# Threshold attention and a gated two-layer network on one core: statistics and first-product sums in other rounds, the exchange of rounds' work rearranged

## The chip, the cores and the metric

The kernel runs on one core of a Trainium2 chip. The metric is the device time of one execution in microseconds. Three runs of the kernel before took 986.61, 984.64 and 983.08 us, median 984.64.

The engines are named as in the profile: PE is TensorE's matrix product and PEld its loading of weights, DVE is VectorE, ACT is ScalarE, POOL is GpSimd, and SP is the queue that issues most DMAs. Every engine executes its own instructions in program order, and semaphores order them against the other engines.

## The reference

Two blocks follow each other. The first is attention with a threshold, over 8 batches and 8 heads of 576 tokens of width 64; the second takes the 4608 tokens of width 512 through 1024 hidden values and back.

```
scores = scale * np.matmul(q, k.transpose(0, 1, 3, 2))
thresh = np.max(scores, axis=-1, keepdims=True) - tau
scores = np.where(scores >= thresh, scores, -1000000000.0)
attn = softmax(scores)
x = np.matmul(attn, v), heads side by side, as 4608 x 512
h = x @ w_in                                   # 512 -> 1024
solu = h * softmax(h)
ln = (solu - mean) / np.sqrt(var + 1e-06) * g_ln
out = ln @ w_out                               # 1024 -> 512
```

The softmax of the second block runs over the 1024 hidden values of a token, and so do the mean and the variance.

## The kernel before

**Rounds.** The work is written out by hand as a loop over rounds. There are 144 slots of scores, 18 to a batch: four pairs of heads, two kinds of tokens and two halves, and two slots for the last 64 tokens of the batch (kind 2, "end tokens"). Round n computes slot n. Its steps are the scores on PE (`scores`, L466) into one buffer `s_ps`; the row maxima on DVE (`maxes`, L488, two per round); the threshold on ACT (`ramp`, L503) and the exponentials (`exps`, L512). One round later GpSimd divides by the sums (`normalise`, L519, L520, L522) and DVE transposes the weights into T (`blocks`, L534). After the second of two slots SP sends T to wT (L543, L545). Three rounds after that slot, PE forms the product with v (`attend_steps`, L576), always in an even round of the steady part, into one half of each of the two banks "o"; ACT copies the result to `xh`, or to `xe` for end tokens (`attended`, L609), and DVE clears that half of the banks for the next product (`clear`, L615), since the product adds to what is there.

**The steady part.** From round 30 (`START`) the second block runs between the scores. An odd round holds half of the second product of one tile of 128 tokens (`ff_o`, L948) into the other half of the banks "o"; its output is copied out by ACT (`ff_out`, L966) and stored by SP (`ff_store`, L987). An even round holds a phase of a first product, then a product with v, then another phase.

**A pair of tiles.** Tokens of two tiles a and b go through the first product together, with seven phases in place of eight blocks. This needs sums of weights, made once, and sums of tokens on GpSimd (`sums_a`, L655, L656 ahead of the first phase's round; `sums_b`, L661, L662 later). The seven phases (`phase`, L691) lie two to an even round, the seventh alone in the fourth even round, so a pair takes 8 rounds. After every two batches one tile of end tokens follows (`one_h`, L715, in four rounds, with one sum on GpSimd, L667). Pairs begin in rounds 30, 38, 50, 58, 66, 74, 86, 94, 102, 110, 122, 130, 138 and 146, single tiles in 46, 82, 118 and 154; round 144 is the first without scores, and what follows is the tail.

**The fence.** The two phases of an even round write the same banks with different rows of PE. So that they don't meet, GpSimd sets a small tile `mark` after the last products of the first phase (`fence`, L110), and the second phase waits for it. GpSimd takes this instruction in its program order like any other.

**The steps behind a pair**, counted in rounds from its start: the halves of h are taken from the banks by ACT (`keep_half`, L730), completed with the other bank by DVE, which gives the row maximum hm (`add_half`, L737), and combined (L746); ACT takes the exponential with its sum (`pair_exp`, L751); DVE multiplies (`pair_mul`, L757) and GpSimd inverts the sum (`ff_sum`, L875, L876). `ff_stats` has mean and variance on DVE (L885, L886) and then five small operations on GpSimd (L889 to L896, "rs chain") that turn them into scale and offset. Then ACT makes V (`ff_norm`, L906), DVE the same values in u (`ff_norm2`, L911), SP exchanges parts (`ff_swap`, L922), DVE transposes to uT (`ff_turn`, L932), and the second product can begin.

**Order in a round.** Jobs are entered in three lists. The program of an even round is: the list `begin`; scores, maxima, thresholds and exponentials; `normalise` of the slot before; the list `middle`; the phases, the fence and the product with v; `blocks` of the slot before; the list `late`; preparation of later heads (scaling L195, copies L201, transposes L209). Since `middle` comes before the phases, what stands in it on GpSimd is ahead of the fence there. `r + n` below is round n of a pair that began in round r; round 8 of a pair is usually round 0 of the next.

## Time and profile before

| | |
|---|---|
| runs | 986.61, 984.64, 983.08 us |
| profiled execution | 984.76 us, span 983.0 us, 1.8 us around it |
| mean granted TensorE clock | 0.961 |
| busy share | PE 85%, DVE 70%, ACT 61%, POOL 58% |
| first score of round 30 to that of round 38 | 174.02 to 221.13 us |
| last score | 891.4 us; the tail lasts to 983.0 |

In a list of waits a line names the waiting engine, what it was to write and its line in the kernel, what released it, and then the total, the number and the longest of the waits in us. In a timeline a line gives the start and the length in us, engine, line, operation, what it writes and reads, and the size; in brackets stands the idle time ahead of it and what ended it. Where several instructions of a kind are joined, "x16" counts them. A product counts two records per multiplication here. In a table by stretch each line is a stretch of time, its length, the busy time of PE, PEld, DVE, ACT and POOL with the number of instructions, the granted TensorE clock (1.00 is full speed), the busy share of the DMA engines and GB/s.

### The profile page before, as it was taken

To read this page: it belongs to the slowest core of one execution; us is meant where nothing else is said; L and a number is where in the kernel's file an instruction comes from. 1 tells how busy PE (TensorE), PEld (TensorE's weight loads), DVE (VectorE), ACT (ScalarE), POOL (GpSimd) and SP (SyncE) were. 2 spreads that over 40 slices of the span, in tenths; PEclk is the share of its full clock that TensorE was granted. 3 is DMA by queue.
4 is the path that set the end of the run, shared out by engine and by line. 5 is a ranking of instruction groups with operands and counts; after the bars stand their busy time and mean duration, and the time that the engine had idled before them with its cause. 6 is when DMAs were issued, how large, how long until landed. Compare 5 with 4: busy or idle time off the path is not lost.

```text
span 983.0 us, 36466 instructions
## 1 busy us (share of the span) xinstructions
PE 838.3 (85%) x15329; PEld 535.9 (55%) x15329; DVE 691.7 (70%) x1403; ACT 599.2 (61%) x1209; POOL 566.2 (58%) x1022
## 2 busy tenths in 40 slices
PE   5668898887978988888987988988888898988996
PEld 3456566543564555555564554555564465555553
DVE  5968788577685776969687677687778577676251
ACT  5868776566664665757665666566666566664131
POOL 3868578647465465756556456475755557565120
PEclk9879999897999999999999999999999999999998
DMA  9999878776766667675767567766687575545111
GB/s 273 251 244 233 206 180 224 196 169 153 197 169 164 168 166 198 174 205 143 211 175 186 150 168 174 186 172 187 163 233 173 142 172 136 155 102 137 35 45 43
DMA packets 83811, 168.57 MB, mean 171 GB/s; under 512 B 15544, under 2 KB 45248, under 8 KB 83648
## 3 DMA queue, kind: packets, MB, share of 16 engines
q1 hardware_dynamic: 82512, 164.25, 65.5%
q8 instruction: 120, 1.97, 0.9%
q10 hardware_dynamic: 1136, 2.00, 0.6%
q14 instruction: 43, 0.35, 0.1%
HBM read 46.14 MB, written 9.44 MB: 57 GB/s over the span
## 4 chain that ended last, share of the span: by engine, by line
PE 38%; DVE 17%; DMA 14%; ACT 9%; issue 9%; POOL 8%; SPq 5%; DVEq 0%; ACTq 0%; POOLq 0%
PE h L691 12%; DMA wT<-T 10%; PE ov L576 8%; PE s_ps L466 6%; DVE w L488 4%; DVE T L534 4%; PE o_ps L948 3%; ACT w L503 3%; DVE bs L885 3%; PE h_ps L841 2%; ACT w L512 2%; PE ov L948 2%; PE h L715 2%; POOL w L522 2%; DVE u L737 2%
## 5 line engine op out<-in xcount | busy, mean ns | idle before, releaser
L488 DVE CUSTOM_DVE_ANT_0 w<-s_ps,tau_t 128x576 f32<-128x576 f32 x282 | 200.8, 749 | 179.5 <-PE s_ps L466 168.9
L503 ACT ACTIVATE w<-s_ps,nth 128x576 f32<-128x576 f32 x282 | 199.3, 742 | 209.5 <-DVE nth L488 203.0
L522 POOL TENSOR_SCALAR w<-w,sm 128x576 f32<-128x576 f32 x288 | 217.8, 768 | 14.3
L512 ACT ACTIVATE w<-w,ntau 128x576 f32<-128x576 f32 x288 | 219.8, 769 | 0.0
L534 DVE STREAM_TRANSPOSE T<-w 128x576 f32<-128x576 f32 x288 | 207.8, 758 | 12.6 <-POOL w L522 10.6
L948 PE MATMUL ov<-w,uT 64*64 64x256 f32 x3456 | 200.4, 376 | 0.0
L466 PE MATMUL s_ps<-kT,qT 64*64 64x512 f32 (+1 forms) x2048 | 173.0, 427 | 16.7 <-ACT w L503 15.4
L948 PEld LDWEIGHTS ov<-w,uT 64*64 64x64 f32 x3456 | 146.3, 133 | 64.6 <-issue 20.5
L576 PE MATMUL ov<-wT,v 64*64 64x128 f32 (+1 forms) x4752 | 141.5, 266 | 42.7 <-ACT ob L966 26.7
L576 PEld LDWEIGHTS ov<-wT,v 64*64 64x64 f32 x4752 | 130.4, 138 | 87.1 <-ACT ob L966 42.7
L519 POOL TENSOR_SCALAR sm<-sm 128x2 f32<-128x2 f32 x144 | 46.3, 322 | 219.7 <-ACT w L512 214.7
L691 PE MATMUL h<-w,xh 64*64 64x512 f32 x896 | 116.2, 623 | 26.1 <-POOL mark L110 15.0
L520 POOL TENSOR_TENSOR sm<-sm,mone 128x2 f32<-128x2 f32 x144 | 103.3, 717 | 12.0
L466 PEld LDWEIGHTS s_ps<-kT,qT 64*64 64x64 f32 x2048 | 70.5, 141 | 53.7 <-ACT w L503 23.2
L691 PEld LDWEIGHTS h<-w,xh 64*64 64x64 f32 x896 | 36.4, 136 | 80.8 <-issue 27.4
L948 PE MATMUL o_ps<-w,uT 64*64 64x256 f32 x1152 | 70.3, 389 | 8.5 <-DVE uT L932 5.4
L906 ACT ACTIVATE V<-u,nb,rs 128x1024 f32<-128x1024 f32 x36 | 44.5, 1236 | 37.3 <-POOL nb L896 27.9
L948 PEld LDWEIGHTS o_ps<-w,uT 64*64 64x64 f32 x1152 | 48.0, 138 | 33.4 <-issue 12.4
L691 PE MATMUL h<-sums,xh 64*64 64x512 f32 x336 | 60.0, 607 | 0.9 <-DVE hm L737 0.5
L691 PE MATMUL h<-k,sum 64*64 64x512 f32 x224 | 58.1, 638 | 0.0
L932 DVE STREAM_TRANSPOSE uT<-V 128x1024 f32<-128x1024 f32 x36 | 43.6, 1212 | 19.2 <-DMA V<-u 13.4
L512 ACT ACTIVATION_READ_ACCUMULATOR w<-w,ntau 128x1 f32 x288 | 56.0, 194 | 0.0
(122 smaller groups left out, 1009.0 us busy)
## 6 DMA issues: line engine op xcount, KB each, us to landing
wT<-T SPq DMA_DIRECT2D x160, 288.0 KB, 6.1
wT<-T SPq DMA_DIRECT2D x64, 576.0 KB, 5.5
V<-u SPq DMA_DIRECT2D x144, 64.0 KB, 2.3
out_dram<-ob SPq DMA_DIRECT2D x71, 128.0 KB, 4.2
q<-in_q_dram SPq DMA_DIRECT2D x24, 288.0 KB, 4.5
qT<-flip SPq DMA_DIRECT2D x48, 144.0 KB, 3.3
q<-in_k_dram SPq DMA_DIRECT2D x24, 288.0 KB, 4.6
kT<-flip SPq DMA_DIRECT2D x48, 144.0 KB, 2.5
```

The source lines that it names most:

```text
L466: nc.tensor.matmul(out=ps[h][ROWS[y], ks], lhsT=lhsT, rhs=d["kT"][ROWS[h], ks], start=True, stop=True,)
L488: nc.vector.tensor_tensor_reduce(out=w, in0=ps[:, 0:S], in1=(zero if loose else tau_t).to_broadcast([P, S]), scale=1.0, scalar=BIG, op0=AL ...
L503: nc.scalar.activation(out=d["w"][x], in_=d["w"][x] if d["loose"] else d["ps"][x][:, 0:S], func=AF.Prelu, bias=d["nth"][x], scale=-1.0, al ...
L512: nc.scalar.activation(out=w, in_=w, func=AF.Exp, bias=ntau, scale=1.0, accum_out=sm[:, x : x + 1])
L519: nc.gpsimd.tensor_scalar(out=sm, in0=sm, scalar1=1e-9, scalar2=None, op0=ALU.add)
L520: nc.gpsimd.tensor_tensor(out=sm, in0=sm, in1=mone, op=ALU.pow)
L522: nc.gpsimd.tensor_scalar(out=w, in0=w, scalar1=sm[:, x : x + 1], scalar2=1.0, op0=ALU.mult, op1=ALU.mult)
L534: nc.vector.transpose(out=T[:, :, r, h, :], in_=w)
L576: nc.tensor.matmul(out=to, lhsT=d["v"][ROWS[u], (h0 + h - u) % 4 if b > 1 else h0 + h, m ^ 4 * u if m < 8 and b < 2 else m,], rhs=rhs, sta ...
L691: mm = nc.tensor.matmul(out=h[ROWS[y], 512 * bank : 512 * bank + 512], lhsT=x[ROWS[r], ROWS[y]], rhs=w[ROWS[r]], start=c == 0 and (n, r, k ...
L906: nc.scalar.activation(out=V, in_=u, func=AF.Identity, bias=nb, scale=rs)
L948: nc.tensor.matmul(out=d["o"][ROWS[z], of : of + 256], lhsT=d["uT"][ROWS[r], m].rearrange("p y x -> p (y x)"), rhs=w2[ROWS[r], m ^ r, 256 ...
```

## The change

- The product with v is drawn from a list of its own (`pv`), of which an even round takes 36 multiplications (72 for end tokens) and the odd round after it the rest. The copy to xh or xe moves to the head of the `begin` list of a later round. `ready`, which lets a pair start, is set so that pairs start in the same rounds.
- The banks are no longer cleared. The first product with v after a new second product has begun in the banks adds to them without a start flag (`both["open"]`), and other products with v begin with one.
- A single phase in an even round (round 6 of a pair, and the second part of a single tile) comes ahead of the product with v.
- `blocks` comes directly behind `normalise`, ahead of `middle`.
- `sums_a` has three operations and moves to `late` of round 0, behind the fence; `sums_b` has one. The third sum, `s2`, shares a buffer with `ident` and `swapped`.
- Copies from the banks and exponentials move to `begin` lists, additions and `pair_mul` to `middle`.
- `ff_stats(a)` moves from `middle` of round 7 to `middle` of round 8, `ff_stats(b)` from round 9 to round 10; norms are in rounds 9 and 12, turns in late 10 and 14. In a single tile the exponential moves to `begin` of round 3.
- `hm` of the halves has two buffers instead of three.

```diff
@@ attend_steps
+        unit["within"] = "open" in both
+        if unit["within"]:
+            assert both["open"] == "fresh"
+            both["open"] = "used"
...
-                            start=m == 0 and "o" not in both, stop=m == NK - 1,
-                            skip_group_check="o" in both,
+                            start=m == 0 and not unit["within"], stop=m == NK - 1,
+                            skip_group_check=unit["within"],
@@ sums
+        both["s2"] = work.tile([P, 2, P], F32, tag="ident", bufs=1, name="sum")
         nc.gpsimd.tensor_tensor(out=both["s"], in0=x2[:, 0:2], in1=x2[:, 2:4], op=ALU.add)
+        nc.gpsimd.tensor_tensor(out=both["s2"], in0=both["s"], in1=x1[:, 0:2], op=ALU.subtract)
         nc.gpsimd.tensor_tensor(out=x2[:, 0:2], in0=x2[:, 0:2], in1=x1[:, 0:2], op=ALU.subtract)
     def sums_b(ts):
-        x1 = tokens(ts[0])
-        nc.gpsimd.tensor_tensor(out=x1[:, 0:2], in0=both["s"], in1=x1[:, 0:2], op=ALU.subtract)
-        nc.gpsimd.tensor_tensor(out=x1[:, 2:4], in0=x1[:, 2:4], in1=x1[:, 0:2], op=ALU.subtract)
+        x = tokens(ts[0])[:, 2:4]
+        nc.gpsimd.tensor_tensor(out=x, in0=x, in1=both["s2"], op=ALU.subtract)
@@ new_pair
-        at(late, 1, first)
-        at(late, 3, second)
-        at(late, 5, lambda: (add_half(a, 1, 1), add_half(b, 1, 0), pair_exp(a)))
-        at(late, 6, lambda: (pair_mul(a), ff_sum(a)))
-        at(middle, 7, lambda: ff_stats(a))
-        at(late, 7, lambda: (keep_half(b, 0, 1), add_half(b, 0, 0), pair_exp(b)))
-        at(begin, 8, lambda: ff_norm(a))
-        at(middle, 8, lambda: (ff_norm2(a), ff_swap(a)))
-        at(late, 8, lambda: (pair_mul(b), ff_sum(b)))
-        at(middle, 9, lambda: ff_stats(b))
-        at(late, 9, lambda: ff_turn(a, r + 9))
-        at(begin, 10, lambda: ff_norm(b))
-        at(middle, 10, lambda: (ff_norm2(b), ff_swap(b)))
-        at(late, 14 if r + 14 <= NS else 11, lambda: ff_turn(b, rnd))
+        at(late, 0, lambda: sums_a(ts))
+        at(begin, 1, first)
+        at(middle, 1, lambda: add_half(a, 0, 1))
+        at(late, 1, lambda: sums_b(ts))
+        at(begin, 3, second)
+        at(middle, 5, lambda: (add_half(a, 1, 1), add_half(b, 1, 0), pair_max(a)))
+        at(begin, 6, lambda: pair_exp(a))
+        at(begin, 7, lambda: keep_half(b, 0, 1))
+        at(middle, 7, lambda: (add_half(b, 0, 0), pair_max(b), pair_mul(a), ff_sum(a)))
+        at(begin, 8, lambda: pair_exp(b))
+        at(middle, 8, lambda: (ff_stats(a), pair_mul(b), ff_sum(b)))
+        at(begin, 9, lambda: ff_norm(a))
+        at(middle, 9, lambda: (ff_norm2(a), ff_swap(a)))
+        at(middle, 10, lambda: ff_stats(b))
+        at(late, 10, lambda: ff_turn(a, rnd))
+        at(begin, 12, lambda: ff_norm(b))
+        at(middle, 12, lambda: (ff_norm2(b), ff_swap(b)))
+        at(late, 14, lambda: ff_turn(b, rnd))
@@ new_one
-        at(late, 2, lambda: (ff_max(t), ff_exp(t)))
-        at(late, 3, lambda: (ff_mul(t), ff_sum(t)))
+        at(late, 2, lambda: ff_max(t))
+        at(begin, 3, lambda: ff_exp(t))
+        at(middle, 3, lambda: (ff_mul(t), ff_sum(t)))
         at(middle, 4, lambda: ff_stats(t))
...
+        at(late, 10 if r < NS else 8, lambda: ff_turn(t, rnd))
@@ o_steps, steady_round
+            if m == 0 and ffn[t]["otag"] is None:
+                both["open"] = "fresh"
             if m + n == 2 * NC:
+                both.pop("open", None)
...
+        pv = []
+        def attend_some(n):
+            key, steps = pv[0]
+            if sum(1 for _ in zip(range(n), steps)) < n or n > 144:
+                pv.clear()
+                begin.setdefault(rnd + 1, []).insert(0, lambda: done_with(key))
         def steady_round(due):
             if (rnd - START) % 2:
+                if pv:
+                    attend_some(145)
                 o_steps(NC)
                 return
...
                     new_pair(ts, rnd)
-                    sums_a(ts)
...
                     new_one(ts[0], rnd)
                     sum_one(ts[0])
...
-            if steps[1:] or steps and rnd >= NS:
+            if steps:
                 steps[0]()
             if due:
                 key = pv_due.pop(0)[1]
-                for _ in attend_steps(key):
-                    pass
-                done_with(key)
-                late.setdefault(rnd + 1, []).append(clear)
+                pv.append((key, attend_steps(key)))
+                attend_some(72 if key[1] == 2 else 36)
             elif rnd >= NS:
                 o_steps(NC // 2 if steps else NC)
-            if steps and rnd < NS or steps[1:]:
-                steps[-1]()
+            if steps[1:]:
+                steps[1]()
@@ the loop over rounds
             if rnd - 1 in live:
                 normalise(rnd - 1)
+                if rnd >= START:
+                    blocks(rnd - 1)
```

More of the change, by code (lines that the diff above doesn't have):

```diff
@@ L66 @@
     small = ctx.enter_context(tc.tile_pool(name="small", bufs=3))
+    signs = work.tile([P, 2 * P], F32, tag="ident", bufs=1, name="ident")
+    ident, swapped = signs[:, 0:P], signs[:, P : P + 64]
     ps_mm = ctx.enter_context(tc.tile_pool(name="ps_mm", bufs=1, space=PSUM))
-    ident = const.tile([P, P], F32, name="ident")
-    swapped = const.tile([P, 64], F32, name="swapped")
     w1 = const.tile([P, NP, DFF], F32, name="w1")
@@ L611, in attended @@
             pairs_free.append(tag)
-    def clear():
-        nc.vector.memset(both["o"].rearrange("p (u n) -> p u n", u=2)[:, :, 0:P], 0.0)
     both = {}
@@ L678, in product @@
             5: lambda: (both["s"][:, c], seven[0, c]),
-            6: lambda: (x1[:, c], seven[1, c]),
+            6: lambda: (both["s2"][:, c], seven[1, c]),
             7: lambda: (x2[:, c], block(0, 1, c)),
@@ L733, in add_half @@
         d = ffn[t]
-        m = small.tile([P, 1], F32, tag=f"hm{g}", name="hm")
+        m = small.tile([P, 1], F32, tag=f"hm{g}", bufs=2, name="hm")
         d["m"].append(m)
@@ L740, in add_half, with pair_max @@
         )
-    def pair_exp(t):
+    def pair_max(t):
         d = ffn[t]
         m, n = d["m"]
-        nm = small.tile([P, 1], F32, tag="hm", name="hm")
+        d["nm"] = nm = small.tile([P, 1], F32, tag="hm", name="hm")
         nc.vector.tensor_scalar(
@@ L748, in pair_exp @@
         )
+    def pair_exp(t):
+        d = ffn[t]
         d["u"] = new_u()
@@ L751, in pair_exp @@
         nc.scalar.activation(
-            out=d["u"], in_=d["x"], func=AF.Exp, bias=nm, scale=1.0, accum_out=d["se"]
+            out=d["u"], in_=d["x"], func=AF.Exp, bias=d["nm"], scale=1.0, accum_out=d["se"]
         )
@@ L770, in first @@
             keep_half(a, 0, 0)
-            add_half(a, 0, 1)
-            sums_b(ts)
         def second():
@@ L797, in at @@
             when.setdefault(r + n, []).append(job)
-        at(late, 2, lambda: (ff_max(t), ff_exp(t)))
-        at(late, 3, lambda: (ff_mul(t), ff_sum(t)))
+        at(late, 2, lambda: ff_max(t))
+        at(begin, 3, lambda: ff_exp(t))
+        at(middle, 3, lambda: (ff_mul(t), ff_sum(t)))
         at(middle, 4, lambda: ff_stats(t))
-        if r < NS:
-            at(begin, 7, lambda: ff_norm(t))
-            at(middle, 7, lambda: (ff_norm2(t), ff_swap(t)))
-            at(late, 10, lambda: ff_turn(t, rnd))
-        else:
-            at(begin, 5, lambda: ff_norm(t))
-            at(middle, 5, lambda: (ff_norm2(t), ff_swap(t)))
-            at(late, 6, lambda: ff_turn(t, rnd))
+        n = 7
+        at(begin, n, lambda: ff_norm(t))
+        at(middle, n, lambda: (ff_norm2(t), ff_swap(t)))
+        at(late, 10 if r < NS else 8, lambda: ff_turn(t, rnd))
         oq.append(t)
@@ L1106, in done_with @@
             if kind == 2 and b % 2:
-                ready.append((rnd + 1, [(b // 2,)]))
+                ready.append((rnd + (rnd < START), [(b // 2,)]))
             elif kind < 2 and hp == NP - 1:
-                ready.append((rnd + 1, [(b, kind, 0), (b, kind, 1)]))
+                ready.append((rnd + (rnd < START), [(b, kind, 0), (b, kind, 1)]))
         def o_steps(n):
@@ L1144, in steady_round @@
                     sum_one(ts[0])
-                    hsteps.append([lambda t=ts[0]: None, lambda t=ts[0]: one_h(t, 0)])
+                    hsteps.append([lambda: None, lambda t=ts[0]: one_h(t, 0)])
                     hsteps.append([lambda t=ts[0]: one_h(t, 1)])
             steps = hsteps.pop(0) if hsteps else []
-            if steps[1:] or steps and rnd >= NS:
+            if steps:
                 steps[0]()
@@ L1162 @@
             if not more and not (
-                ready or cur or prev or between or pv_due or live or oq or hsteps or ojob
+                ready or cur or prev or between or pv_due or live or oq or hsteps or ojob or pv
                 or max([rnd - 1, *begin, *middle, *late]) >= rnd
@@ L1172 @@
                 both["h"], both["o"] = take("h2")[1], take("ov")[1]
-                clear()
                 oq.append(prev)
```

## The prediction

> **What bounds the kernel now.** I read the page's busy shares first, then TensorE's waits, then the timeline around two beginnings of a pair, and last a table by stretch. The steady part (rounds 30 to 143) decides.

> The page's first part, and then TensorE's waits (us in total, times, longest):

> ```profile
> PE 838.3 (85%) x15329; PEld 535.9 (55%) x15329; DVE 691.7 (70%) x1403; ACT 599.2 (61%) x1209; POOL 566.2 (58%) x1022
> ```

> ```profile
> PE h L691 <- DVE hm L737: 29.2, 24, 2.0
> PE ov L576 <- ACT ob L966: 26.7, 15, 2.9
> PE s_ps L466 <- ACT w L503: 16.3, 18, 2.4
> PE h L691 <- POOL mark L110: 15.0, 11, 3.4
> ...
> PE ov L576 <- DMA wT<-T: 9.6, 14, 2.0
> ...
> PE o_ps L948 <- DVE uT L932: 5.4, 2, 5.0
> PE h L691 <- ACT u L730: 4.7, 13, 0.4
> PE ov L576 <- DVE ov L615: 3.5, 3, 1.4
> ```

> TensorE is busy 85% and is the only engine without slack; what it waits for is short and many-sided. The change aims at hm, ob, wT and ov. The line to watch is the fourth: the fence on GpSimd, only 15.0 us now.

> An ordinary beginning of a pair (round 74, from 454.46), from the timeline:

> ```profile
> 454.46 1.16 PE L466 MATMUL s_ps<-kT,qT 64*64 64x64 f32 x16
> 456.10 0.24 POOL L201 COPY qe<-qT 128x64 f32<-128x64 f32 x1
> 457.37 0.72 DVE L488 CUSTOM_DVE_ANT_0 w<-s_ps,tau_t 128x576 f32<-128x576 f32 x1
> 460.82 0.09 POOL L110 MEMSET mark<- 128x1 f32 x1
> 460.96 1.95 PE L691 MATMUL h<-w,xh 64*64 64x512 f32 x16 [0.65 <-POOL mark L110]
> 461.56 1.18 DVE L757 TENSOR_TENSOR u<-u 128x1024 f32<-128x1024 f32 x1
> 461.84 1.00 POOL L201 COPY qe<-qT 128x64 f32<-128x64 f32 x1
> ```

> The one beginning in which the statistics of an earlier tile stand ahead of the fence (round 86, from 531.18):

> ```profile
> 534.43 1.28 DVE L885 BATCH_NORM_STATS2 bs<-u 128x6 f32<-128x512 f32 x2
> 536.07 0.34 POOL L889 TENSOR_SCALAR rs<-mv,se 128x1 f32<-128x1 f32 x1 [0.96 <-DVE mv L886]
> 537.75 0.26 POOL L896 TENSOR_SCALAR nb<-mv,rs 128x1 f32<-128x1 f32 x1
> 539.44 0.10 POOL L110 MEMSET mark<- 128x1 f32 x1
> 539.59 3.25 PE L691 MATMUL h<-w,xh 64*64 64x512 f32 x16 [3.38 <-POOL mark L110]
> 542.59 1.60 PE L466 MATMUL s_ps<-kT,qT 64*64 64x64 f32 x16
> ```

> Here GpSimd waits for DVE's mv, does five small operations and two sums, and only then sets the mark. TensorE stands 3.38 us, and the next phase takes 3.25 us where 1.95 is usual. The table by stretch says why (time; PE, PEld, DVE, ACT, POOL busy; granted clock; DMA):

> ```profile
> 536.20:539.50 3.30, 0.01 (x2) 0.00 (x0) 1.06 (x2) 0.94 (x3) 2.87 (x8) 1.00 0.34 69
> 540.10:543.50 3.40, 3.40 (x28) 1.22 (x24) 0.00 (x0) 0.00 (x0) 3.13 (x6) 0.50 0.94 252
> ```

> After the standstill the granted clock is 0.50 for one stretch of about 3.4 us: from this phase (539.59) to the second product (which starts at 544.02) it takes 4.43 us instead of 1.77+0.97 = 2.74, so a long wait costs another 1.7 us.

> **The change, part by part.** The unit is a pair of token tiles: 8 rounds. From starts of undisturbed instructions in the timeline: scores 0.97, phase 1.77, product with v 1.96, half a second product 3.45. So 8×0.97 + 7×1.77 + 4×1.96 + 4×3.45 = 41.8 us without waits. Measured from score start to score start: seven ordinary periods 49.48, 49.29, 50.54, 52.8, 48.54, 49.52, 48.15, mean 49.8; the first after a single tile 53.0, 51.3, 51.1, mean 51.8; single tiles (21.6 without waits) 29.0, 26.2, 26.2, mean 27.1; rounds 30 to 38 47.1, rounds 38 to 46 52.6.

> *The split.* An even round asks for 36 multiplications of a unit that has 9×2×2 = 36 (72 of 72 for the end tokens; the profile counts two records each): the whole product stays in the even round and the odd one only finds the end. What really moves is the copy to xh or xe: to the head of ScalarE's next even round, where it waits for the half second product before it. The pairs begin at the same rounds. I price it between −1 and +1 us a pair and take 0: 0.37 us of copy beside 0.97 of scores and 1.77 of a phase, which cover it.

> *No clearing.* 60 memsets of 0.272 = 16.3 us of DVE go; only the 3.5 us wait on L615 was on the path.

> *Order in a round.* The phase of round 6 and the single tile's product now come ahead of the product with v and cover its wait for ob (26.7 us in 15). T directly behind the normalising sends wT's DMAs ahead of the middle list (1.4 us by stats and T), past nothing but itself on SP; the 12 us on wT goes. Copies and exponentials at a round's begin and the additions in the middle list end most of hm: 0.6 a pair is left (1.94 in the rows of round 2). All this is the gain: 49.8 − 41.8 = 8.0 a pair now, of which 0.7 stays (0.6 hm, 0.1 in round 6).

> *Sums.* One operation (0.73) more ahead, one less behind, and all three behind the fence: 0.7 to 1.4 us off GpSimd ahead of the mark. This is inside the next step.

> *Statistics in even rounds: the cost.* stats(a) moves from round 7 to round 0 of the next pair, stats(b) from round 1 to round 2. There GpSimd does normalise, the rs chain, the reciprocal of the sums, and then the fence that the second phase waits for. Round 0, from its score start E: DVE begins its maxes at E+2.7 (457.37−454.46 = 2.91 now; the list it carries from round 7 is alike), maxes 1.36, T 1.42, stats 1.49: mv at E+7.0. pair_mul (1.18) follows on DVE at once. While it runs GpSimd stands: L201 took 1.00 beside it and 0.24 without it. So the chain (0.34+0.23+0.58+0.19+0.26 with gaps, 536.07 to 538.01 = 1.94) begins about 0.8 late or at its end, 8.15; it ends at 10.1, the two operations on se 0.8, mark 0.1: E+10.9. Naturally TensorE is there at 0.97+1.77+1.96 = E+4.7. Wait 6.2; bounds 3.6 (the row of round 86 with its 0.18 of pipelined end) and 7. Round 2 has a lighter list and no pair_mul: maxes from E+2.2, then 1.36+1.42+1.49+0.11+1.94+0.1 = E+8.6 against 4.7 and 0.6 of hm: 3.3; bounds 0 and 3.6. The slow stretch behind: 1.7 in round 0, and 1.3 in round 2, a wait nearer to one stretch, where not every alignment is punished (3.10 at 310.95 was: 3.31 us for the phase; 2.87 and 2.68 elsewhere were not).

> [...]

> *Ordinary period after:* 41.8 + 0.7 + 6.2 + 1.7 + 3.3 + 1.3 = 55.0, against 49.8: +5.2, eight times (58, 66, 74, 94, 102, 110, 130, 138) = +41.6. Rounds 38 to 46: 55.0 − 52.6 = +2.4. First after a single tile: its statistics stand in round 0, without pair_mul, and nothing in round 2: 41.8 + 4.3 + 1.7 + 1.0 = 48.8, −3.0, three times = −9.0. Single tile: its sum comes behind the same chain (10.8 + 0.73 = E+11.5), and its product needs it at 0.97+1.96+1.1 = E+4.0: wait 7.5, 21.6+7.5+1.7 = 30.8 against 27.1, three times = +11.1. Rounds 30 to 38 have no statistics ahead: −3 (0 to −5.3). Tail: −5 (0 to −10): the last tile's 5.02 us wait for uT and its slow product shrink.

> Later turns (10, 14), norms (9, 12), two hm buffers and the shared buffer of ident cost 0: the tiles' second products begin in the same rounds, covered by 8 rounds of lag; without that cover an uT wait of 1.2 a tile.

> Sum: 41.6+2.4−9.0+11.1−3−5 = +38.1. Against the profiled execution's 984.76 us (span 983.0, 1.8 around it, 0.1 above the median of the runs): 1022.9, taken as 1023.

> **The rivals.**
> *R1, faster: the fence waits only as the row of round 86 does (3.6 + 1.7) and not at all in round 2*, because DVE, 16 us lighter and with lists spread, gets to its maxes early. Period 41.8+0.7+5.3 = 47.8 (−2.0×8), rounds 38 to 46 −4.8, first after single −3.7×3, single 26.8 (−0.3×3), −3, −5: −41, 944. For it: that row is the only direct one. Against it: there GpSimd waited for one tile's statistics with DVE early (533.10, E+1.9), without pair_mul or se. It decides where fence waits and slow stretches of an ordinary pair come to less than 8.3 us instead of my 12.5 (9 periods of 42.5+X against 451.0, others +5.9 lower).
> *R2, a trade:* X near 8.3: 976 to 1002, about 985.
> *R3, worse:* both waits at their upper bounds and both punished in full, X = 7+3.6+1.7+1.7 = 14, the single tiles +1 each: 1039 and more, up to 1060 if the copy at the head of the even round holds the maxes' ramps too.
> *The split is real* (half of a product lands in the odd round): then even rounds are 1 us shorter ahead of the fence and the wait is 1 longer: the same time.

> **How the numbers follow.** My forecast 0.68, its own range 1003 to 1036; R1 0.17 (932 to 975); R2 0.07; R3 0.08. The range of 8 in 10 takes my case, R2 and the nearer part of R1: 968 to 1037. About 0.3% (3 us) is what a measurement can tell from no change. Slower: 0.68+0.08+0.01 = 0.77; same 0.04 (the middle of R2); faster 0.17+0.02 = 0.19.

> **What would show it.** TensorE's waits: fence about 95 us (15.0 now), the single tile's product on its sum about 20, hm about 6, ob and wT next to none, no L615 memset; granted clock 0.5 behind the fence in most even rounds 0. Wrong if the fence stays under 50 us, if DVE's maxes in round 0 begin before E+1.5, or if hm stays where it is.

## The result, and the profile after

The changed kernel takes 1025.43 us (median; 1021.05 to 1030.83) beside 983.86 us (979.69 to 986.61) for the kernel before: 1.0429 times as long, 95% interval 1.0354 to 1.0504. The profiled execution took 1021.31 us with a span of 1019.5, that is 36.5 us more span than before; the sum on record said 38.1. Two kernels below, the one with statistics in odd rounds and the one with T early in odd rounds as well, were profiled in a slower execution than most of theirs (932.67 us beside a median of 919.88, and 995.30 beside 985.88), so I use waits and lengths of rounds of these two profiles, and no total time.

TensorE's longest waits in the changed kernel, from the list of waits:

```profile
PE h L694 <- POOL mark L110: 80.9, 22, 5.7
PE s_ps L466 <- ACT w L503: 18.3, 19, 3.1
PE h L718 <- POOL sum L670: 12.0, 4, 4.7
PE ov L582 <- ACT ob L971: 10.8, 9, 1.6
PE ov L582 <- DMA wT<-T: 6.2, 9, 2.1
...
PE h L694 <- DVE hm L740: 2.5, 3, 1.1
```

The many short waits of before are mostly gone (hm 29.2 to 2.5, ob 26.7 to 10.8), and one wait has grown past all of them: the fence, 15.0 to 80.9 us.

The beginning of the pair of round 66 (408.42), from the timeline:

```profile
410.77 0.72 DVE L488 CUSTOM_DVE_ANT_0 w<-s_ps,tau_t 128x576 f32<-128x576 f32 x1
...
412.10 1.43 DVE L534 STREAM_TRANSPOSE T<-w 128x576 f32<-128x576 f32 x2
...
413.46 1.24 DVE L890 BATCH_NORM_STATS2 bs<-u 128x6 f32<-128x512 f32 x2
...
414.86 1.17 DVE L763 TENSOR_TENSOR u<-u 128x1024 f32<-128x1024 f32 x1
415.05 1.20 POOL L894 TENSOR_SCALAR rs<-mv,se 128x1 f32<-128x1 f32 x1 [2.42 <-DVE mv L891]
...
418.78 0.10 POOL L110 MEMSET mark<- 128x1 f32 x1
...
418.93 3.69 PE L694 MATMUL h<-w,xh 64*64 64x512 f32 x16 [5.21 <-POOL mark L110]
```

Maxes, T and statistics stand one behind the other on DVE; GpSimd waits 2.42 us for mv, then needs 3.7 us to the mark, and TensorE waits 5.21 us in all. The table by stretch (columns as before) gives the clock after it:

```profile
418.05:424.88 6.83, 5.95 (x40) 2.13 (x44) 0.30 (x1) 1.67 (x2) 6.40 (x13) 0.50 0.22 60
```

From the spans and records I worked out, for the rounds with scores from 30 on (174.6 to 933.4 us in the profile after), how long TensorE was idle and how much of its busy time lay in stretches at 0.50, half of which counts as lost: idle 93.7 to 122.3 us, lost to the clock 17.1 to 37.4 us, the rest 606.5 to 599.1. So 41.4 us more there: 28.6 of waiting, 20.3 of clock, 7.4 given back. A phase takes 1.95 us by its records and 1.77 from start to start, so 0.18 us of its end is covered where no gap follows; 33 fewer gaps (89 to 56) would by this be 6 of the 7.4, an estimate.

### The profile page after: what moved, and what is told of

Read it like the earlier page. It is cut to its first block, busy times and chain, and to the rows that moved or that the text cites. A ratio compares the mean times of both kernels' runs of the same rounds, so it can differ in the third digit from the quotient of the medians.

```text
span 1019.5 us, 36371 instructions
## 1 busy us (share of the span) xinstructions
PE 846.6 (83%) x15329; PEld 523.6 (51%) x15329; DVE 670.9 (66%) x1343; ACT 600.8 (59%) x1209; POOL 560.6 (55%) x1022
## 4 chain that ended last, share of the span: by engine, by line
PE 39%; DVE 22%; POOL 10%; DMA 10%; ACT 9%; issue 7%; SPq 2%; DVEq 0%; ACTq 0%; POOLq 0%
PE h L694 12%; PE s_ps L466 8%; DVE T L534 7%; PE ov L953 7%; DMA wT<-T 6%; DVE w L488 5%; ACT w L503 3%; ACT w L512 3%; PE o_ps L953 3%; PE ov L582 3%; DVE bs L890 3%; PE h_ps L846 2%; POOL rs L894 2%; DMA v<-in_v_dram 2%; POOL rs L898 2%
## 5 line engine op out<-in xcount | busy, mean ns | idle before, releaser
L488 DVE CUSTOM_DVE_ANT_0 w<-s_ps,tau_t 128x576 f32<-128x576 f32 x282 | 201.6, 751 | 267.1 <-PE s_ps L466 218.1
L503 ACT ACTIVATE w<-s_ps,nth 128x576 f32<-128x576 f32 x282 | 199.8, 743 | 148.2 <-DVE nth L488 144.4
L522 POOL TENSOR_SCALAR w<-w,sm 128x576 f32<-128x576 f32 x288 | 213.7, 754 | 14.3
L466 PE MATMUL s_ps<-kT,qT 64*64 64x512 f32 (+1 forms) x2048 | 178.3, 435 | 20.0 <-ACT w L503 17.5
L953 PEld LDWEIGHTS ov<-w,uT 64*64 64x64 f32 x3456 | 141.6, 134 | 72.9 <-issue 29.8
L694 PE MATMUL h<-w,xh 64*64 64x512 f32 x896 | 129.4, 694 | 59.4 <-POOL mark L110 57.6
L582 PEld LDWEIGHTS ov<-wT,v 64*64 64x64 f32 x4752 | 126.1, 134 | 62.5 <-issue 26.3
L582 PE MATMUL ov<-wT,v 64*64 64x128 f32 (+1 forms) x4752 | 135.0, 260 | 22.5 <-ACT ob L971 10.8
L466 PEld LDWEIGHTS s_ps<-kT,qT 64*64 64x64 f32 x2048 | 68.1, 146 | 62.7 <-issue 29.5
L694 PEld LDWEIGHTS h<-w,xh 64*64 64x64 f32 x896 | 38.5, 151 | 115.2 <-POOL mark L110 60.1
L733 ACT COPY u<-h 128x512 f32<-128x512 f32 x56 | 31.4, 587 | 111.0 <-PE h L694 111.0
L911 ACT ACTIVATE V<-u,nb,rs 128x1024 f32<-128x1024 f32 x36 | 44.6, 1240 | 53.2 <-POOL nb L901 50.1
L894 POOL TENSOR_SCALAR rs<-mv,se 128x1 f32<-128x1 f32 x36 | 24.8, 689 | 84.3 <-DVE mv L891 84.2
```

Source lines behind the costliest of these rows:

```text
L466: nc.tensor.matmul(out=ps[h][ROWS[y], ks], lhsT=lhsT, rhs=d["kT"][ROWS[h], ks], start=True, stop=True,)
L488: nc.vector.tensor_tensor_reduce(out=w, in0=ps[:, 0:S], in1=(zero if loose else tau_t).to_broadcast([P, S]), scale=1.0, scalar=BIG, op0=AL ...
L503: nc.scalar.activation(out=d["w"][x], in_=d["w"][x] if d["loose"] else d["ps"][x][:, 0:S], func=AF.Prelu, bias=d["nth"][x], scale=-1.0, al ...
L522: nc.gpsimd.tensor_scalar(out=w, in0=w, scalar1=sm[:, x : x + 1], scalar2=1.0, op0=ALU.mult, op1=ALU.mult)
L582: nc.tensor.matmul(out=to, lhsT=d["v"][ROWS[u], (h0 + h - u) % 4 if b > 1 else h0 + h, m ^ 4 * u if m < 8 and b < 2 else m,], rhs=rhs, sta ...
L694: mm = nc.tensor.matmul(out=h[ROWS[y], 512 * bank : 512 * bank + 512], lhsT=x[ROWS[r], ROWS[y]], rhs=w[ROWS[r]], start=c == 0 and (n, r, k ...
```

## The experiments

All ratios are to the kernel before, run beside it on the same chip, with the 95% interval. The medians of the kernel before lie between 980.3 and 984.9 us from one set of runs to the next, so a difference in us between two changed kernels of different sets can be off by some us; the ratios are the better measure there. E is the start of a round's first score, "the mark" the start of the memset that is the fence.

### Statistics alone, in the kernel before

```diff
-        at(middle, 7, lambda: ff_stats(a))
...
-        at(begin, 8, lambda: ff_norm(a))
-        at(middle, 8, lambda: (ff_norm2(a), ff_swap(a)))
+        at(middle, 8, lambda: ff_stats(a))
...
-        at(middle, 9, lambda: ff_stats(b))
...
+        at(begin, 9, lambda: ff_norm(a))
+        at(middle, 9, lambda: (ff_norm2(a), ff_swap(a)))
+        at(middle, 10, lambda: ff_stats(b))
+        at(late, 10, lambda: ff_turn(a, rnd))
...
```

> The kernel before, with only the statistics moved as in the change (statistics of a in round 8, of b in round 10, norms in 9 and 12, turns late in 10 and 14; in the tail the single tile's norm and turn in 7 and 8). My theory (this move alone is enough for the loss): the mark of round 0 comes at about E+9.4 instead of E+6.4, a wait of 4.8 instead of 0.65 and a slow stretch of 1.7 to 2.6, round 2 0.8 more: 5 to 8 us a period, 1025 to 1065 us, fence wait 60 to 100 us. Rival (the loss needs the other parts, above all pair_mul beside the chain or the lists at begin): 975 to 1000.

Measured: 1025.99 us, 1.0454 (1.0399 to 1.0508). The fence leads TensorE's waits:

```profile
PE h L691 <- POOL mark L110: 60.1, 21, 4.5
```

The mark of round 0 comes at E+9.7 (mean of eight pairs; E+6.35 before). The move alone is enough for a loss of the observed size. But the changed kernel has parts that win, as the runs below show, so it needn't be all of the loss there.

### The chain behind the fence

```diff
-        at(middle, 8, lambda: (ff_stats(a), pair_mul(b), ff_sum(b)))
+        at(middle, 8, lambda: (ff_stats(a), pair_mul(b)))
+        at(late, 8, lambda: (ff_chain(a), ff_sum(b)))
...
         at(middle, 10, lambda: ff_stats(b))
+        at(late, 10, lambda: ff_chain(b))
...
         at(middle, 4, lambda: ff_stats(t))
+        at(late, 4, lambda: ff_chain(t))
...
```

`ff_stats` keeps DVE's three operations here, and `ff_chain` has GpSimd's five.

> The changed kernel, with one thing moved: the five small GpSimd operations of the statistics (rs chain) and the reciprocal of the sums stand behind the round's phases and fence (late list) in rounds 8 and 10 of a pair, 4 of a single tile; DVE's part stays. My theory (the fence queued behind the rs chain is the whole loss): TensorE's wait for the fence falls from 80.9 us to under 15, the wait of the single tile's product from 12.0 to under 3, the stretches at granted clock 0.50 behind the fence go, and the time falls to 920 to 955 us, under both kernels. Rival (DVE is the late one and the chain only shows it): fence wait goes, but waits on hm, ob or wT come in its place, 970 to 1000. Rival (the copies and exponentials at a round's begin are the loss): 1000 to 1030.

Measured: 990.4 us, 1.0104 (1.0064 to 1.0144): 35 us less than the change, not 70 to 105. The fence wait is 0.2 us, but this stands at the head of the list:

```profile
PE h L694 <- DVE hm L740: 50.4, 14, 4.8
```

The first rival is what happened, with a chain of its own. From the timeline of this kernel (rounds 58 to 60):

```profile
363.17 1.24 ACT L918 ACTIVATE V<-u,nb,rs 128x1024 f32<-128x1024 f32 x1 [3.60 <-POOL nb L908]
...
369.04 1.50 DVE L534 STREAM_TRANSPOSE T<-w 128x576 f32<-128x576 f32 x2 [6.39 <-POOL w L522]
...
371.16 0.68 DVE L740 CUSTOM_DVE_ANT_0 u<-h,u 128x512 f32<-128x512 f32 x1
...
372.00 1.99 PE L694 MATMUL h<-k,sum 64*64 64x512 f32 x8 [4.59 <-DVE hm L740]
```

Behind the fence GpSimd now does the chain, se and three sums before it normalises slot 58. DVE's T of that slot is the next in its queue and stands 6.39 us; the addition that TensorE needs is queued behind T, although its own input is long there. This made T's early place a suspect.

### pair_mul beside the chain

```diff
-        at(middle, 8, lambda: (ff_stats(a), pair_mul(b), ff_sum(b)))
+        at(middle, 8, lambda: (pair_mul(b), ff_stats(a), ff_sum(b)))
```

> The changed kernel with pair_mul of b ahead of the statistics of a in round 8, no longer beside the rs chain. If DVE's two-input product holds GpSimd's operations (in the changed kernel the first of the chain took 1.20 us beside it), the chain only starts as late as it could go on before: the first operation takes 0.35 again, the mark comes within 0.3 us of where it was, 1018 to 1030 us. If it doesn't hold them: the mark comes 1.2 us later in each of 10 rounds, 1033 to 1040.

Measured: 1026.68 us, 1.0471 (1.039 to 1.0552). The first operation of the chain, in the list of groups, in the change and then in this kernel:

```profile
L894 POOL TENSOR_SCALAR rs<-mv,se 128x1 f32<-128x1 f32 x36 | 24.8, 689 | 84.3 <-DVE mv L891 84.2
```

```profile
L894 POOL TENSOR_SCALAR rs<-mv,se 128x1 f32<-128x1 f32 x36 | 12.6, 350 | 103.3 <-DVE mv L891 103.2
```

It takes 350 ns when pair_mul is out of the way, and the mark comes at E+10.63 instead of E+10.38. Delaying the chain by pair_mul's whole length costs 0.25 us: beside it GpSimd had been held for nearly as long. So the 0.8 us of hold in the prediction's working stands.

### A real split

```diff
-                attend_some(72 if key[1] == 2 else 36)
+                attend_some(36 if key[1] == 2 else 18)
```

> The changed kernel, with 18 (36 for end tokens) multiplications of a product with v in the even round, so that half of it really lands in the odd round. My theory (the even round's fence comes at a time that GpSimd sets; TensorE only waits 1 us longer for it, and the odd round is 1 us longer): fence wait 80.9 + 17 to 25 us, the time the same or up to 12 us more, 1020 to 1037. Rival (a product with v in two parts fills a wait elsewhere): 1005 to 1017.

Measured: 1053.14 us, 1.0728 (1.0668 to 1.0788), 28 us above the change: the direction of the theory, and more than twice its upper bound of 12. The fence wait is 98.6 (+17.7, as expected), the single tile's product waits 17.0 for its sum (+5.0), and the loss to the clock goes from 37.4 to 46.9, which I had left out. The odd rounds of ordinary pairs take 0.9 to 1.3 us more, while rounds 0 and 2, whose ends the fence sets, change by −0.5 and +0.1 only.

### Statistics of b in an odd round

```diff
-        at(middle, 10, lambda: ff_stats(b))
+        at(middle, 11, lambda: ff_stats(b))
```

> The changed kernel with only the statistics of b one round later, in round 11, an odd one without fence. Theory (each statistics ahead of a fence costs what I priced it at): the fence wait in round 2, 2.65 to 2.87 us a pair, and its slow stretch go, 9 to 10 pairs: 25 to 35 us less, 990 to 1002. Rival (the wait moves on to hm, ob or uT, or to the fence of round 4): over 1010.

Measured: 1034.4 us, 1.0537 (1.047 to 1.0605): no gain, and about 9 us more than the change. The wait and slow stretch of round 2 are gone as expected (seven ordinary pairs: idle 2.76 to 0.00 us in rounds 2 and 3), but most of it comes back in the same pairs: 0.98 in rounds 4 and 5, 2.52 instead of 1.22 in rounds 6 and 7, so that an ordinary pair takes 53.9 us instead of 54.4. The rest of the time is lost elsewhere: first pairs after single tiles take 53.2 instead of 50.2, single tiles 30.4 instead of 29.2, the tail 90.1 instead of 86.1; the clock loss is 46.2 instead of 37.4. The rival holds. Part of the way shows in the groups of ScalarE: V of b is at the head of round 12's list and, with its values only made in round 11, all V wait 77.7 us for nb (50.1 in the change); exponentials wait 21.4 us for the DMA of the exchange (10.4). What makes the first pairs and the tail longer stays open.

### The order of the phases, and then T with it, in the kernel before

```diff
-            if steps[1:] or steps and rnd >= NS:
+            if steps:
                 steps[0]()
...
-            if steps and rnd < NS or steps[1:]:
-                steps[-1]()
+            if steps[1:]:
+                steps[1]()
```

> The kernel before, with only the order of the phases taken from the change: the single phase of round 6 and the single tile's second part ahead of the product with v. Theory (the wait for ob, 26.7 us in 15, stands mostly there and is covered by 1.77 us of phase): ob wait under 12 us, time 962 to 976. Rival (the next wait, hm in round 0 or wT, takes the place): 979 to 987.

Measured: 959.42 us, 0.9758 (0.9685 to 0.9831): below the theory's range. ob has gone from TensorE's longer waits; the wait for wT has grown from 9.6 to 21.1. The next kernel has this and, in addition,

```diff
                 normalise(rnd - 1)
+                if rnd >= START:
+                    blocks(rnd - 1)
```

> The kernel before with two parts of the change: the order of the phases (which alone gave 959.4 us and left a wait of 21.1 us for wT and 31.3 for hm) and the transposes T ahead of the middle list. Theory: T and so wT's DMAs go out 1 to 1.5 us earlier, the wait for wT falls under 10 us, hm stays or grows by up to 10 since the middle list comes later on DVE; 945 to 957 us. Rival (T, queued on DVE before the middle list, waits for GpSimd's normalising and holds the statistics, so that fence or hm take all of it): 958 to 970.

Measured: 1000.14 us, 1.019 (1.0125 to 1.0256). The wait for wT is 10.3 us, as hoped, but the time is 41 us more than without T's early place, worse than either theory. The way is the rival's: T stands for GpSimd's normalising 37.6 us in all instead of 10.2, here with T early and then without:

```profile
L534 DVE STREAM_TRANSPOSE T<-w 128x576 f32<-128x576 f32 x288 | 210.4, 765 | 37.6 <-POOL w L522 37.6
```

```profile
L534 DVE STREAM_TRANSPOSE T<-w 128x576 f32<-128x576 f32 x288 | 207.8, 758 | 12.0 <-POOL w L522 10.2 <-DMA V<-u 0.8 <-DMA wT<-T 0.5
```

The statistics stand behind T, the rs chain behind the statistics. The marks of rounds 0 and 2 come at E+7.83 and E+8.00 instead of 6.36 and 6.32, and the fence wait is 25.6 us instead of 4.1.

### T's place in the changed kernel

Taken back in all rounds:

```diff
                 normalise(rnd - 1)
-                if rnd >= START:
-                    blocks(rnd - 1)
```

> The changed kernel with only the transposes T back at their old place, behind the phases and ahead of the late list. Theory (T's 1.42 us of DVE stand ahead of the statistics, which hold the fence): the mark of rounds 0 and 2 comes 1.4 us earlier, fence wait 80.9 to 50 to 62 us, less at granted clock 0.50, against 6 to 15 us more of waits for wT; 990 to 1012 us. Rival (the gain on wT is as large as what T costs the fence, as I priced it): 1018 to 1030.

Measured: 966.3 us, 0.9842 (0.9784 to 0.99): without this one line the change is faster than the kernel before. Its TensorE waits:

```profile
PE h L694 <- POOL mark L110: 49.4, 22, 3.9
PE ov L582 <- DMA wT<-T: 17.1, 28, 2.1
```

The fence waits 31.5 us less, wT 10.9 us more. The marks come at E+8.59 and 6.19 (change: 10.38 and 7.49), and the loss to the clock is 28.3 us (37.4). ob, 10.8 us in the change, is gone from the waits: those of ScalarE's 28 exponentials, of which one of a pair stands ahead of a copy to ob, fall from 34.0 to 10.9 us.

Early in even rounds alone:

```diff
-                if rnd >= START:
+                if rnd >= START and rnd % 2 == 0:
                     blocks(rnd - 1)
```

> The changed kernel with T ahead of the middle list in even rounds only. This tells in which rounds T's early place costs the 59 us that taking it back in all rounds won. Theory (in even rounds T stands directly ahead of the statistics, and the mark comes 1.0 to 1.5 us later in rounds 0 and 2; in odd rounds it only holds the additions, the exponential of round 6 and by it ob): most stays, 1000 to 1018 us, fence wait 65 to 80, ob wait under 4. Rival (odd rounds alone, as in the kernel with statistics in odd rounds, where T there cost 66): 962 to 975.

Measured: 1012.92 us, 1.0336 (1.0277 to 1.0395), fence wait 77.5 us. The marks of rounds 0 and 2 come at E+9.96 and 7.51, 1.4 and 1.3 us later than with T late, as expected. By the ratios, of the 5.9% that T's place costs in the change, 4.9% come from the even rounds, where T stands directly ahead of the statistics; the remaining 1% is no larger than the intervals. The expected end of ob did not come (10.2 us).

### Statistics in odd rounds

```diff
+        at(late, 5, lambda: pair_exp(a))
+        at(late, 6, lambda: (pair_mul(a), ff_sum(a)))
+        at(middle, 7, lambda: (ff_stats(a), add_half(b, 0, 0), pair_max(b)))
+        at(late, 7, lambda: pair_exp(b))
+        at(late, 8, lambda: (pair_mul(b), ff_sum(b)))
+        at(middle, 9, lambda: (ff_norm2(a), ff_swap(a), ff_stats(b)))
...
-                if rnd >= START:
+                if rnd >= START and rnd % 2 == 0:
                     blocks(rnd - 1)
```

(The first addition of a pair stands first in its list, and the single tile's statistics are in round 5; all else is as in the change.)

> The changed kernel with both statistics in odd rounds (a in 7, b in 9, single tile in 5), exponentials and products as early as in the kernel before, the first addition at the head of its list, and T ahead of the middle list in even rounds only; phase order, no clearing, sums behind the fence, norms and turns as in the change. Theory (the rest of the change is sound, and only the statistics ahead of the fence made it slow): fence wait under 15 us, hm under 15, period of a pair 44 to 47 us, 915 to 945 us. Rival (DVE or GpSimd, with 40 us and more of work in a period, set the pace in odd rounds): 950 to 980.

Measured: 919.88 us, 0.9358 (0.9282 to 0.9434): 6.4% less than the kernel before, the fastest here. The fence wait is a little over the expected 15 us:

```profile
PE h L694 <- POOL mark L110: 17.3, 13, 2.0
```

In rounds 0 and 1 of ordinary pairs TensorE is idle 0.08 us and loses nothing to the clock (change: 5.51 and 2.09). With T early in odd rounds as well:

> The kernel with statistics in odd rounds, with T ahead of the middle list in every round as in the change, no longer in even rounds alone. Theory (in odd rounds T sends no DMA and only holds the additions and the statistics, and by them GpSimd and the next fence): fence wait in round 2 from 0.7 to 2.0 us to 2 to 3.5, time 930 to 950 us. Rival (T's place is indifferent where the statistics aren't ahead of a fence): 915 to 925.

Measured: 985.88 us, 1.0059 (1.0019 to 1.0099), 66 us more and 36 above the theory's range. Here the odd rounds hold the statistics, and here T's place costs in the odd rounds: the mark of round 2 comes at E+9.73 instead of 6.51. The fence wait is 42.1 us, and hm, absent before, 14.5: the additions stand behind T as well. With the run before this shows what matters: not even or odd, but T ahead of what a fence, or a phase, waits for in the end.

### A dose on the fence

Six idle operations on GpSimd are put ahead of the fence of round 0, in the kernel with statistics in odd rounds:

```diff
+    def slow_pool():
+        for _ in range(6):
+            nc.gpsimd.tensor_tensor(out=mark, in0=mone[:, 0:1], in1=mone[:, 0:1], op=ALU.pow)
...
+        at(middle, 8, slow_pool)
```

> The kernel with statistics in odd rounds, with six idle operations of 0.57 us on GpSimd (about 3.9 us start to start) in the middle list of round 8 of each pair, that is ahead of the fence of a next pair's round 0 (twelve times in the rounds with scores): a dose of the delay alone, on a kernel in which DVE and ScalarE are as early as can be. Theory (late fence and slow stretch behind it are the cost, 3.4 to 3.9 us of wait and 1.3 to 2.6 of clock each): 45 to 80 us more, 965 to 1000. Rival (other engines catch up in the wait, and the rest of the period gives it back): under 955.

Measured: 986.66 us, 1.0034 (0.9992 to 1.0077), 67 us more. One of the places, from the timeline:

```profile
348.42 4.26 POOL L767 TENSOR_TENSOR mark<-mone 128x1 f32<-128x1 f32 x6
352.75 0.10 POOL L110 MEMSET mark<- 128x1 f32 x1
...
352.90 2.95 PE L694 MATMUL h<-w,xh 64*64 64x512 f32 x16 [3.89 <-POOL mark L110]
```

In ordinary pairs rounds 0 and 1 have 3.84 us of idle time (0.08 without the dose) and lose 1.82 us to the clock (0): 5.6 us each, and twelve of them would be 67. Rounds 2 to 7 of these pairs are idle as long as without the dose (3.75 and 3.76 us), so nothing is given back there. That the product meets the difference so exactly is partly luck: three of the doses fall on single tiles, which take 27.7 us instead of 23.1, and the pairs behind those take 44.8 instead of 46.9. For a wait of 3.8 us, the price that the prediction used, the wait plus one slow stretch, is right.

## Why the prediction was right, and where it was not

**Right by its main mechanism.** The fence is queued behind the statistics' chain on GpSimd, TensorE waits for it in rounds 0 and 2 of each pair, and behind the longer wait the granted clock is 0.50 (at 418.05 to 424.88, behind 5.21 us). The dose measures the price alone; the chain behind the fence ends the fence wait; the statistics alone in the kernel before are enough for 4.5%.

**Term by term**, for an ordinary pair: 49.8 to 54.4 us was measured over seven pairs, 55.0 forecast.

| | forecast | measured |
|---|---|---|
| wait in round 0 | 6.2 | 5.5 |
| clock behind it | 1.7 | 2.1 |
| wait in round 2 (fence and hm) | 3.9 | 2.8 |
| clock behind it | 1.3 | 0.45 |
| round 6 | 0.1 | 1.2 |
| ordinary pair, before to after | +5.2 | +4.7 |
| rounds 38 to 46, before to after | +2.4 | +3.2 |
| first pair after a single tile, before to after | −3.0 | −1.6 |
| single tile | +3.7 | +2.1 |
| rounds 30 to 38 | −3 | −2.6 |
| tail, from the last score | −5 | −5.4 |

The two sizes that were off in round 2 go the same way: the mark came at E+7.5 instead of E+8.6, since DVE's maxes begin at E+1.3 there and not at E+2.2 (mean of eight pairs), and only two of seven such waits were followed by a slow stretch. For round 0 DVE began at E+2.1 instead of E+2.7.

That the sum came within 2 us is partly luck: the three single tiles were each forecast 1.6 us too dear and the three first pairs each 1.4 too cheap, and these errors cancel. The waits that were named came out shorter than forecast: the fence 80.9 us for about 95, the single tile's product 12.0 for about 20, hm 2.5 for about 6.

**Wrong in the step "Order in a round".** It credited T's early place with the wait for wT, 12 us (the row beside it says 9.6), and a gain. The gain on wT is there (17.1 to 6.2 us in the changed kernel), but undoing the same line saves 59 us, more than the whole loss. My sum had T's 1.42 us in the chain of rounds 0 and 2 without saying that it is this line that puts it there; that is 2.84 us a pair before any clock, and I never set it against the 12 us. So the time came out right while the cause was told only in half: the statistics in even rounds are one part (44 us alone in the kernel before), T ahead of them the other, and the rest of the change is a gain. Changed kernel without T's early place: 0.984. The kernel before with the statistics alone: 1.045. The difference, 6%, is what phase order, no clearing, sums behind the fence and earlier lists bring together; the order of the phases alone brings 2.4% in the kernel before. How the remainder is shared among the others was not tried one by one.

**Also wrong in that step:** ob was to vanish, and T was to send wT's DMAs "past nothing but itself on SP". 10.8 us of ob stayed. ScalarE's copy to ob stands behind the exponential of a at the head of round 6; in round 72 that one waited 1.75 us for the DMA of the exchange (it starts at 456.62), and then TensorE waited 1.48 us for ob. This exchange (V from u) belongs to tile b of the pair before, in its round 12, and SP now issues it behind wT:

```profile
447.45 0.57 SPq L543 DMA_DIRECT2D wT<-T  x1
448.07 2.92 SPq L545 DMA_DIRECT2D wT<-T  x2
451.08 3.21 SPq L927 DMA_DIRECT2D V<-u  x4
```

With T back at its old place the order in the same round is the other:

```profile
424.26 3.17 SPq L927 DMA_DIRECT2D V<-u  x4
427.54 0.62 SPq L543 DMA_DIRECT2D wT<-T  x1
428.20 3.03 SPq L545 DMA_DIRECT2D wT<-T  x2
```

The exponentials' waits for the exchange and TensorE's for ob go together: 10.4 and 10.8 us in the change, 8.9 and 10.2 with T early in even rounds alone, none of either with T late. One transfer sent earlier made another of the same queue late: V<-u is issued from 451.08, behind wT's from 447.45.

**The rivals.** R1 (944, fence waits as short as in round 86 and none in round 2) was wrong on the fence; what it says of the rest of the change was not: with the statistics out of the fence's way, exponentials and the first addition earlier and T early in even rounds only, the kernel takes 920 us. That the split is in name only was right (in the changed kernel practically all records of a product with v stand in the even round), but its real form is not "the same time": it costs 28 us. The even rounds with a late fence hardly get shorter, the odd rounds get longer by the half product, which that line left out, and the longer waits lose 9.5 us more to the clock.

**The resolution.** The prediction took 0.3% as the least difference that can be told; the intervals here are ±0.4 to 0.75%.

## What to carry to other kernels

An instruction that releases the bottleneck (here a memset of 0.1 us, for which TensorE waited 3.89 us behind 4.26 us of idle operations) is as late as everything ahead of it in its own queue, and as everything that those wait for on other engines: follow that chain back over all engines before pricing a reordering. Price each reordered line by what it pushes back as well as by the wait that it ends; the early transposes ended 11 us of waits, and the kernel without them is 59 us faster. And when a sum comes out right, undo its parts one at a time all the same: here that found a kernel 6.4% faster than the one before.

## What the runs showed of the hardware

```profile
431.71:435.12 3.41, 1.17 (x44) 0.93 (x36) 2.94 (x5) 1.35 (x4) 1.30 (x4) 1.00 0.61 134
435.12:438.53 3.41, 2.92 (x16) 1.05 (x20) 0.00 (x0) 0.00 (x0) 3.05 (x8) 0.50 0.99 278
486.32:489.73 3.41, 2.17 (x76) 1.93 (x68) 3.38 (x6) 2.24 (x6) 0.99 (x3) 1.00 0.76 218
489.73:493.14 3.41, 2.00 (x28) 0.89 (x32) 0.48 (x1) 0.00 (x0) 2.88 (x9) 1.00 0.99 267
493.14:496.55 3.41, 3.41 (x66) 2.10 (x60) 2.34 (x6) 2.56 (x5) 1.35 (x2) 1.00 0.90 238
```

The first wait leaves PE idle for 2.24 us of one window, and the next is at 0.50. The second is cut by the grid into 1.24 and 1.41 us, and nothing follows. Counted over the rounds with scores from 30 on of these two profiles (174.0 to 892.6 and 174.6 to 933.4 us), with idle time as the records have it: of the windows at full speed, those with 2.0 us or more idle were followed by a slow one in 23 of 23 cases, those with less than 1.3 in none of 328, and those between in 5 of 41. Six of the 23 were idle throughout, the other 17 were not. Of the 39 slow windows, the 11 with 0.78 us or more idle were followed by another, and the 28 with 0.55 or less by full speed.

Behind waits of 5.2 to 5.7 us I had counted one slow stretch of 3.4 us; in the profile after, seven of the eight were 6.83 us long, and in these the wait reaches into the first slow window (0.88 us idle in 418.05 to 421.46). Part of the first thus lies in the wait itself, so that the loss was 1.5 to 3.0 us and not 1.7.

**An operation on GpSimd took longer beside pair_mul on DVE.** In the profile after, the first operation of the chain (L894) lies beside pair_mul (1.17 us, two inputs) in 14 of its 36 places, by 0.91 to 0.98 us, and takes 1.12 to 1.20 us there; in 21 of the other 22 it takes 0.34. With pair_mul ahead of the chain its mean is 350 ns instead of 689, and the mark comes 0.25 us later only. The runs show these times, and not what holds the operation.
